# One more drain instruction on GpSimd, ahead of the last indirect scatter of an attention and mixture-of-experts kernel

## The chip, the cores and the metric

The kernel runs on one core of one Trainium2 chip. The metric is the device time of the program in microseconds; lower is better. A change is compared with the kernel before on the same chip.

## What is computed

Attention for 8 batches of 8 heads, 1152 keys of width 64 and 576 queries (each the mean of two neighbouring query rows), followed by a mixture of 8 experts on the 4608 tokens of width 512 that come out. Each token goes to one expert, the one with the largest gate.

```python
q_pool = q.reshape(B, H, S // 2, 2, D).mean(axis=3)
attn = softmax(scale * q_pool @ k.T)          # per batch and head
x = (attn @ v)                                # as 4608 rows of 512
logits = x @ w_gate + modality_bias[modality_id]
e_idx = argmax(logits);  gate_w = softmax(logits)[e_idx]
for e in range(8):
    rows = e_idx == e
    out[rows] = gate_w[rows] * (relu(x[rows] @ w1[e]) @ w2[e])
```

## The kernel before

**Two phases.** `attention` goes through 32 pairs of heads and writes the 4608 rows of x to a DRAM tensor `xs`, together with the gate and a scale of each row. `Router` works out for each row its expert and makes two lists of row numbers for blocks of 256 rows that belong to one expert: `giA`, `siA` for the first six blocks and `giB`, `siB` for the others. `experts` then works block by block.

**A block.** `load_x` gathers its rows from `xs` with two indirect DMAs of 128 rows each (`gather_x`, line 1173). These are issued by GpSimd (POOL), as are all indirect DMAs of the kernel. `load_w` fetches the expert's weights through SyncE's queue, `split_w` splits each weight piece into a high and a low half (ScalarE and VectorE, lines 1268 and 1269), `gemm1` and `gemm2` are the two matrix products on TensorE, `scaled` multiplies the result by the gate on ScalarE (`o`, line 1339), and `scatter` writes 128 rows of `o` to the rows of the output that `siA` or `siB` names, with an indirect DMA on GpSimd (line 1342).

**The order.** `run_blocks` writes out 18 full blocks by hand, all engines of the phase in the order of the code (`manual_schedule`). The first half of a block is scattered at its end (`scatter(j, 0)`), the second half five steps into the next block. After the loop stand the second half's scatter of the last full block (`scatter(order[-2], 1)`) and the split of the last weight piece. Then comes `block(NBF)`, a half block of 128 rows: `half_gemm1` makes the first product with rows and columns exchanged and turns it back with transposes (lines 1304 to 1316), `gemm2` makes the second (lines 1331 to 1333), `scaled` and `scatter` follow. That scatter is the last indirect DMA of the program.

**What is queued on GpSimd at the end.** In order: the two scatters of the last full block, the scatter of the half block, a load of a count from SBUF and a branch on it (lines 1426 and 1427; the count is 0 here, so the blocks of the conditional part are passed over), waits until every software-issued DMA has landed, one INC_SWDGE_SEM, which sets the semaphores of the software DMAs to what the passed-over branch would have left, and the program's end (line 1541): a drain on every engine, a barrier of all engines, a clearing of semaphores and a second barrier. Apart from this end, the only drain on GpSimd stands in the program's first microsecond (line 1533).

Of the kernel before, what the change touches and what calls it, by code (L numbers as in the profile page):

```python
# [156 lines left out]
def drain(g):  # L157
    for _ in g:
        pass
# [998 lines left out]
def index(rt, j, h):  # L1158
    (gi, si), k = (rt.idxA, 2 * j) if j < NA else (rt.idxB, 2 * (j - NA) if j < NBF else 2 * (NBF - NA) + j - NBF)
    return gi[:, k + h:k + h + 1], si[:, k + h:k + h + 1]  # L1160
# [38 lines left out]
def experts(tc, ctx, rt, ident, pre, w1, w2, out, side, first):  # L1199


    nc = tc.nc
# [20 lines left out]
    def load_x(j):  # L1223
        B.setdefault(j, {})["xg"] = gather_x(nc, rt, j, lambda h: xq.tile([P, XW], F32, name=f"xg{h}", bufs=1))

    def turn_x(j):

        b = B[j]
        b["gate"] = xp.tile([P, 2], F32, name="gate", bufs=3)
        b["xh"], b["xl"] = (xq.tile([P, 2, 4, P], F16, name="xpart", bufs=6) for _ in range(2))  # L1230
        for h in parts(j):
            x, sc = b["xg"][h][:, 0:DM], b["xg"][h][:, DM + 1:XW]
            nc.vector.tensor_copy(b["gate"][:, h:h + 1], b["xg"][h][:, DM:DM + 1])
            xh, xl = (xq.tile([P, DM], F16, name="xs", bufs=4) for _ in range(2))
            nc.scalar.activation(xh, x, AF.Copy, scale=sc)
            nc.vector.scalar_tensor_tensor(xl, x, sc, xh, op0=ALU.mult, op1=ALU.subtract)
            b["xs", h] = xh, xl
        yield
        for h in parts(j):
            for o, x in zip((b["xh"], b["xl"]), b["xs", h]):  # L1240
                nc.sync.dma_start_transpose(out=o[:, h], in_=x)
        yield

    def load_w(j, q):

        b = B.setdefault(j, {})
        e = b.get("e")
        if e is None:
            own, k = (rt.ownA, j) if j < NA else (rt.ownB, j - NA) if j < NBF else (rt.ownH, j - NBF)
            e = b["e"] = nc.sync.value_load(own[0:1, k:k + 1], min_val=0, max_val=E - 1)  # L1250
        if q < 4:
            t = wr.tile([P, 4, TB], F32, name="w1r", tag="w")
            nc.sync.dma_start(out=t.rearrange("p c f -> p (c f)"), in_=w1[bass.ds(e, 1), q].rearrange("a p n -> p (a n)"))
        else:
            t = wr.tile([P, 2, DM], F32, name="w2r", tag="w")
            nc.sync.dma_start(out=t.rearrange("p c f -> p (c f)"), in_=w2[bass.ds(e, 1), q - 4].rearrange("a p n -> p (a n)"))
        b["r", q] = t

    def split_w(j, q):
        b = B[j]  # L1260
        t = b["r", q]
        shape, nm = ([P, 4, TB], "w1") if q < 4 else ([P, 2, DM], "w2")
        if q < 4:
            i = next(slot) % W1B
            hi, lo = (pre.tile(shape, F16, name=f"{nm}{x}{i}") if i < NF else wp1.tile(shape, F16, name=nm + x) for x in "hl")
        else:
            hi, lo = (wp2.tile(shape, F16, name=nm + x) for x in "hl")
        nc.scalar.activation(hi, t, AF.Copy, scale=WSC)
        nc.vector.scalar_tensor_tensor(lo, t, WSC, hi, op0=ALU.mult, op1=ALU.subtract)
        b["w", q] = (hi, lo)  # L1270
# [65 lines left out]
    def scaled(j, h):  # L1336
        b = B[j]
        o = b["o", h] = xp.tile([P, DM], F32, name=f"o{h}")
        nc.scalar.activation(o, b["po"][h], AF.Copy, scale=b["gate"][:, h:h + 1])

    def scatter(j, h):
        nc.gpsimd.indirect_dma_start(out=out[:, :], out_offset=bass.IndirectOffsetOnAxis(ap=index(rt, j, h)[1], axis=0),  # L1342
                                     in_=B[j]["o", h][:, :], in_offset=None, bounds_check=T - 1, oob_is_err=False)
# [16 lines left out]
    def run_blocks():  # L1360

        todo = iter(pieces[NF:])

        def fetch(n=1):
            for _ in range(n):
                p = next(todo, None)
                if p:
                    load_w(*p)

        fetch(WR)  # L1370
        load_x(1)
        for q in range(NF, 4):
            split_w(0, q)
        turn = {1: turn_x(1)}
        fetch(4)
        late = order.index(NA)
        ahead, own = {}, {}
        for m in range(1, len(order)):
            own[m] = T_OWN[m == late] if m in (1, late) else ()
            ahead[m] = () if m in (1, late) else T_AHEAD  # L1380
        for i, j in enumerate(order[:-1]):
            for s in range(8):
                k = 8 * i + 7 + s
                if i == 0 and s < 4:
                    split_w(0, 4 + s)
                    fetch()
                (gemm1 if s < 4 else gemm2)(j, s % 4)
                for _ in range(own[i + 1].count(s)):
                    next(turn[i + 1], None)
                if k > 7:  # L1390
                    split_w(*pieces[k])
                    fetch()
                if i and s == T_ST:
                    scatter(order[i - 1], 1)
                if i + 2 < len(order) and i + 2 != late:
                    if s == GX:
                        load_x(order[i + 2])
                        turn[i + 2] = turn_x(order[i + 2])
                    for _ in range(ahead[i + 2].count(s)):
                        next(turn[i + 2])  # L1400
            drain(turn[i + 1])
            scaled(j, 0)
            scaled(j, 1)
            scatter(j, 0)
            if i + 2 == late:
                drain(side)
                load_x(order[i + 2])
                turn[i + 2] = turn_x(order[i + 2])
        scatter(order[-2], 1)
        split_w(*pieces[-1])  # L1410

    def block(j):
# [10 lines left out]
    with tc.manual_schedule(engines=MAN0):  # L1423
        run_blocks()
        block(NBF)
# [120 lines left out]
```

## Time and profile before

| | us |
|---|---|
| median of three runs | 1149.84 |
| lowest, highest | 1148.15, 1151.22 |
| the profiled execution, its own time | 1147.58 |
| its span, from the first to the last instruction | 1145.8 |
| outside the span in that execution | 1.78 |

The profile names an engine's sequencer with a q (POOLq): its instructions (waits, branches, drains) occupy the engine's queue but not the engine. A row of a view by source line gives an operation, how often it ran, the shortest, median and longest duration in ns, and the start of the first and of the last one in us from the span's start.

### The profile page before, as it was taken

The page shows a single profiled execution, that of the slowest core. Times are in us where ns is not written, and L with a number is a line of the kernel's source. Part 1 is how long each engine was busy: PE and PEld are TensorE (multiplying, and loading weights), DVE is VectorE, ACT ScalarE, POOL GpSimd, SP SyncE. Part 2 cuts the span into 40 slices and gives each one's busy share as a digit, 9 for nine tenths or more (in the row PEclk, how much of TensorE's full clock was granted, in tenths as well). Part 3 has the DMA queues.
Part 4 walks back from the last instruction along what each step waited for, and adds up shares of the span by engine and source line. Part 5 has one row for each costly group of instructions (what it writes and reads, how often), then busy time and mean ns, then how long its engine had stood idle before and what let it go on. Part 6 is the DMA issues. An engine that isn't in the chain of part 4 may idle for free. (4 is left out here: it accounts for less than half of the span.)

```text
span 1145.8 us, 36648 instructions
## 1 busy us (share of the span) xinstructions
PE 1109.3 (97%) x15001; PEld 816.3 (71%) x15001; DVE 978.9 (85%) x1962; ACT 915.3 (80%) x1463; POOL 419.5 (37%) x408
## 2 busy tenths in 40 slices
PE   7999999999999999999999989999999999999995
PEld 3777777777777777777777767866676666766763
DVE  7999999999999999999999999888977667576661
ACT  5999999999999999999999989765656565565561
POOL 7753534444343454434445331232213221211201
PEclk9999999999999999999999999999999999999998
DMA  7776867857858759669668453699989999989970
GB/s 230 204 178 166 190 178 166 196 158 165 194 148 201 190 149 206 152 164 207 165 167 186 129 129 85 226 269 273 287 259 294 291 289 275 280 267 289 263 233 22
DMA packets 175568, 232.65 MB, mean 203 GB/s; under 512 B 92351, under 2 KB 126799, under 8 KB 175392
## 3 DMA queue, kind: packets, MB, share of 16 engines
q1 hardware_dynamic: 169254, 210.45, 70.3%
q0 software_dynamic: 6128, 19.78, 6.4%
q8 instruction: 119, 1.95, 0.7%
q14 instruction: 57, 0.47, 0.2%
q10 hardware_dynamic: 10, 0.00, 0.0%
HBM read 146.11 MB, written 19.18 MB: 144 GB/s over the span
## 5 line engine op out<-in xcount | busy, mean ns | idle before, releaser
L881 ACT ACTIVATE Pe<-psc 128x432 int32<-128x432 f32 x768 | 377.9, 526 | 43.1 <-PE psc L880 34.2
L813 DVE TENSOR_REDUCE mp<-pm 128x1 f32<-128x512 f32 x566 | 372.6, 684 | 14.4 <-PE pm L812 7.2
L938 PE MATMUL xp<-VH,Pe 128*128 128x65 f16 x2880 | 372.6, 193 | 0.0
L940 PE MATMUL xp<-VS,Pl 128*128 128x65 f16 x2880 | 371.9, 193 | 0.4 <-DVE Pl L864 0.4
L939 PE MATMUL xp<-vl,Pe 128*128 128x64 f16 x2880 | 370.7, 192 | 0.0
L939 PEld LDWEIGHTS <-Pe 128*128 128x128 f16 x2880 | 267.6, 98 | 87.6
L879 PE MATMUL psc<-B 128*128 128x432 f16 (+2 forms) x1152 | 304.0, 286 | 1.7 <-ACT Pe L881 1.5
L880 PE MATMUL psc<-B 65*128 65x432 f16 (+2 forms) x1152 | 304.7, 287 | 0.5 <-DMA B<-mr 0.5
L938 PEld LDWEIGHTS <-Pe 128*128 128x128 f16 x2880 | 271.9, 98 | 45.2 <-issue 7.0
L940 PEld LDWEIGHTS <-Pl 128*128 128x128 f16 x2880 | 266.5, 97 | 0.6 <-DVE Pl L864 0.5
L862 ACT ACTIVATE Pl<-Pe 128x1152 f16<-128x1152 uint16 (+1 forms) x190 | 219.3, 1154 | 6.0
L812 PE MATMUL pm<-hi,QB 128*128 128x512 f16 x566 | 213.7, 379 | 8.4 <-DVE mp L813 8.1
L674 POOL TENSOR_TENSOR lo<-rawk,hi 128x576 f16<-128x576 f32 (+1 forms) x68 | 88.0, 1298 | 196.0 <-ACT hi L658 185.6
L761 POOL TENSOR_SCALAR VH<-rawv,sc 128x512 f16<-128x512 f32 (+1 forms) x60 | 103.5, 1735 | 153.0 <-PE xp L940 73.7
L1287 PE MATMUL ph<-xpart,w1l 128*128 128x256 f16 x544 | 148.3, 273 | 0.0
L1285 PE MATMUL ph<-xpart,w1h 128*128 128x256 f16 x544 | 148.3, 273 | 0.0
L1286 PE MATMUL ph<-xpart,w1h 128*128 128x256 f16 x544 | 148.3, 273 | 0.0
L880 PEld LDWEIGHTS <-B 65*128 65x128 f16 x1152 | 112.9, 98 | 25.2 <-issue 2.5
L879 PEld LDWEIGHTS <-B 128*128 128x128 f16 x1152 | 112.5, 98 | 9.2 <-issue 3.8
L1291 DVE SCALAR_TENSOR_TENSOR hl<-ph,hh 128x512 f16<-128x512 f32 x72 | 49.7, 690 | 77.0 <-ACT hh L1290 76.3
L1290 ACT ACTIVATE hh<-ph 128x512 f16<-128x512 f32 x72 | 43.0, 598 | 87.2 <-PE ph L1287 87.2
L1333 PE MATMUL po<-w2h,hl 128*128 128x512 f16 x296 | 112.2, 379 | 0.0
(263 smaller groups left out, 1921.2 us busy)
## 6 DMA issues: line engine op xcount, KB each, us to landing
w2r<-in_w_dram SPq DMA_DIRECT2D x76, 512.0 KB
w1r<-in_w_dram SPq DMA_DIRECT2D x72, 512.0 KB
rawv<-in_att_dram SPq DMA_DIRECT2D x32, 576.0 KB
B<-hi SPq DMA_DIRECT2D x128, 144.0 KB
rawq<-in_att_dram SPq DMA_DIRECT2D x31, 576.0 KB
rawk<-in_att_dram SPq DMA_DIRECT2D x31, 576.0 KB
B<-qh SPq DMA_DIRECT2D x128, 72.0 KB
B<-lo SPq DMA_DIRECT2D x64, 144.0 KB
```

The lines of the kernel that those rows point to most:

```text
L812: nc.tensor.matmul(pm, QB[p % 2][:, u], s["hi"][:, t * 512:(t + 1) * 512], start=True, stop=True)
L813: nc.vector.tensor_reduce(mp[:, u, t:t + 1], pm, op=ALU.max, axis=AX.X)
L862: nc.scalar.activation(low, rest, AF.Copy, scale=LOW)
L879: nc.tensor.matmul(o, b1[:, ks], b1[:, qs], start=True, stop=False, skip_group_check=True)
L880: nc.tensor.matmul(o, b2[:, ks], b2[:, qs], start=False, stop=True, skip_group_check=True)
L881: nc.scalar.activation(Pe[:, D + x0:D + x1], pt, AF.Exp, scale=1.0 / 16)
L938: nc.tensor.matmul(out, Ph[:, qs], vh[:, c, j, 0:D + 1], start=c == 0 and g == 0, stop=False, skip_group_check=True)
L939: nc.tensor.matmul(out[:, 0:D], Ph[:, qs], vl[:, c, j], start=False, stop=False, skip_group_check=True)
L940: nc.tensor.matmul(out, Pl[:, qs], vs[:, c, j, 0:D + 1], start=False, stop=c == NKC - 1, skip_group_check=True)
L1285: nc.tensor.matmul(o, hi[:, c, fs], xh[:, :, c], start=c == 0, stop=False)
L1286: nc.tensor.matmul(o, hi[:, c, fs], xl[:, :, c], start=False, stop=False)
L1287: nc.tensor.matmul(o, lo[:, c, fs], xh[:, :, c], start=False, stop=c == 3)
```

## The change

After the second half's scatter of the last full block, GpSimd gets one drain. It is written between two statements that stand there already:

```diff
         scatter(order[-2], 1)
+        nc.gpsimd.drain(fusable=False)
         split_w(*pieces[-1])
```

`split_w` issues nothing on GpSimd, so in GpSimd's queue the drain stands directly behind that scatter and directly in front of what belongs to the half block's scatter (a register move, a wait for the landing of the scatter in front, and the transfer itself). The drain waits for no semaphore and updates none. No other instruction of GpSimd or of another engine is added, removed or moved, and no wait changes its semaphore or its value. Line numbers behind the place rise by one: the program's end is line 1542 there, and the count and its branch are lines 1427 and 1428.

## Prediction

> **What bounds the kernel now.** I read the busy times by stage first, with the borders put where the half block begins and where its last work ends.
>
> ```profile
> core 0: us, PE busy (x) PEld busy (x) DVE busy (x) ACT busy (x) POOL busy (x), PEclk, DMA share, GB/s
> 0.00:700.00 700.00, 681.72 (x11499) 520.73 (x11500) 667.19 (x1487) 647.12 (x1098) 325.96 (x321) 1.00 0.71 173
> 700.00:1120.00 420.00, 415.97 (x3425) 287.88 (x3424) 308.76 (x471) 263.13 (x355) 90.64 (x85) 1.00 0.94 263
> 1120.00:1134.00 14.00, 11.59 (x81) 7.72 (x79) 2.92 (x5) 5.02 (x12) 2.34 (x3) 1.00 0.11 41
> 1134.00:1145.80 11.80, 0.00 (x0) 0.00 (x0) 0.00 (x0) 0.00 (x0) 0.59 (x1) 0.65 0.01 3
> ```
>
> TensorE is busy for 682 of the first 700 us and for 416 of the next 420. So the bulk is bound by TensorE, and a GpSimd instruction can do nothing for it. The last row is different: for 11.8 us no engine computes, apart from 0.59 us on POOL, and almost nothing moves (3 GB/s). Here the end of the program is set by queues alone, and that stretch is the one to take apart.
>
> The instructions of POOL and ACT around it, in order of time (start, duration):
>
> ```profile
> 1123.92 0.97 POOL L1342 DMA_INDIRECT out_dram<-o,siB  x1 [2.52 <-ACT hh L1306]
> 1133.61 0.97 POOL L1342 DMA_INDIRECT out_dram<-o,siB  x1 [8.72 <-ACT o L1339]
> ...
> 1132.65 0.69 ACT L1339 ACTIVATE o<-po,gate 128x512 f32<-128x512 f32 x1 [4.86 <-PE po L1333]
> ```
>
> The last scatter is issued at 1133.61, after `o` is ready at 1132.65 + 0.69 = 1133.34. Between the end of the scatter in front (1123.92 + 0.97 = 1124.89) and 1133.34 POOL has nothing to do: 8.45 us. What follows the last scatter on the sequencers stands in the views of two lines, the branch (L1427) and the program's end (L1541):
>
> ```profile
> L1427 POOLq EVENT_SEMAPHORE  x5: 17/43/1421, 1134.9 to 1136.6; - x5
> ...
> L1427 POOLq INC_SWDGE_SEM  x1: 1720/1720/1720, 1136.7 to 1136.7; - x1
> ...
> L1541 SPq EVENT_SEMAPHORE  x14: 17/28/28, 1138.4 to 1145.7; - x14
> L1541 POOLq EVENT_SEMAPHORE  x4: 17/17/17, 1144.8 to 1145.7; - x4
> L1541 POOLq DRAIN  x3: 40/107/6286, 1138.5 to 1145.3; - x3
> L1541 SPq DRAIN  x3: 7/7/13, 1139.1 to 1145.0; - x3
> L1541 DVEq DRAIN  x2: 17/72/128, 1132.1 to 1145.4; - x2
> L1541 PEldq DRAIN  x2: 8/8/8, 1133.7 to 1145.1; - x2
> L1541 ACTq DRAIN  x2: 8/8/8, 1136.5 to 1145.0; - x2
> ...
> L1541 POOLq EVENT_SEMAPHORE_RANGE_CLEAR  x1: 177/177/177, 1145.1 to 1145.1; - x1
> ```
>
> In order of time: POOL's waits for the landings, the longest 1.421 us, end at 1136.6; INC_SWDGE_SEM takes 1.720 us from 1136.7 and ends at 1138.4; then comes the first of POOL's three drains, from 1138.5. It must be the one of 6.286 us: POOL's first semaphore instruction of the end starts at 1144.8 = 1138.5 + 6.3, and the two later drains lie in the 1.0 us behind it. All other engines had come to their first drain long before: DVE at 1132.1, PE at 1133.7, ACT at 1136.5, SP at 1139.1. The barrier waits for POOL's drain alone. It is 6.286 us on the path that ends the program, 0.55% of the span, with no engine at work.
>
> **What the drain does in that time.** It doesn't wait for a transfer: all landings were waited for by 1136.6, in front of it. It doesn't wait for an instruction of the engine either, since POOL's last one ended at 1133.61 + 0.97 = 1134.6. And it isn't the price of a drain as such, since the next two take 0.107 and 0.040 us. The fourth drain of POOL in the program stands at its beginning, before any DMA:
>
> ```profile
> L1533 POOLq INC_SWDGE_SEM  x1: 31/31/31, 0.2 to 0.2; - x1
> ...
> L1533 POOLq DRAIN  x1: 169/169/169, 0.4 to 0.4; - x1
> ```
>
> 0.169 us. So the long one is the only drain that has software DMAs behind it which no drain has yet followed. These are the transfers issued by POOL:
>
> ```profile
> xs<-x POOLq DMA_DIRECT2D x1, 576.0 KB, 7.5
> ...
> xg<-xs,giB POOLq DMA_INDIRECT x25, 5.8
> out_dram<-o,siB POOLq DMA_INDIRECT x25, 5.3
> out_dram<-o,siA POOLq DMA_INDIRECT x12, 6.0
> xg<-xs,giA POOLq DMA_INDIRECT x10, 5.8
> ...
> rawq<-xs,giA POOLq DMA_INDIRECT x2, 6.8
> ...
> xs<-gt POOLq DMA_DIRECT2D x1, 9.0 KB, 6.8
> ```
>
> 1 + 25 + 25 + 12 + 10 + 2 + 1 = 76. My theory: a drain on POOL goes through a record of each software DMA that it hasn't closed before, and the end pays for what has gathered: 6.286 / 76 = 0.083 us each, if all 76 are still there (more each, if some were closed on the way).
>
> **The change, part by part.** It adds one instruction on POOL; nothing else is issued, removed or moved. Two costs and two gains come from it.
>
> *The new drain itself.* It stands behind the scatter that ends at 1124.89. Bounds for its length are the shortest drain, 0.040 us, and the long one, 6.286 us. I take 6.286, because 75 of the 76 transfers lie in front of it, as in the row of the long one. Queued behind it on POOL is only the last scatter with its register move and wait; who waits for that is the end of the program. If the drain starts at 1124.9, it ends at 1131.2, and `o` is ready at 1133.34: hidden, with 2.1 us left. It may first have to see the scatter in front landed, and the chain that ended last shows when POOL's queue saw that:
>
> ```profile
> 1123.92 2.73 DMA out_dram<-o,siB
> 1126.65 0.02 issue
> 1126.67 0.02 POOLq L1342
> 1126.69 6.69 issue
> 1133.38 0.02 POOLq L1426
> ```
>
> The wait for that landing passed at 1126.67. A drain that starts there ends at 1126.7 + 6.3 = 1133.0, still 0.3 us before 1133.34. So it costs nothing on the path: the cover is TensorE's second product of the half block and `o`, and each microsecond beyond the cover would come back in full.
>
> *The long drain at the end.* By the theory it has one record left, so it becomes as short as a drain with little to do: 0.107 us, the median of the three. Then it is not the last any more: SP is next. SP's drains of the first barrier begin at 1139.1 and it has three of 7 to 13 ns, the second of them about 0.1 us behind the first. POOL would be through at 1138.5 + 0.1 = 1138.6, the barrier waits for SP until about 1139.3 and not for POOL until 1144.8. The gain is 1144.8 - 1139.3 = 5.5 us, which is less than the 6.2 us taken from the drain, because SP's chain behind the last semaphores (12 waits at some 60 ns, from 1138.4 to 1139.1) now ends last.
>
> *INC_SWDGE_SEM.* SP's first wait of the end is over at 1138.4, just when INC_SWDGE_SEM ends, so both POOL and SP hang on that one. It took 1.720 us here and 0.031 at the program's beginning, where no software DMA had been issued. If it too works through what has gathered, the new drain shortens it, and all of what it saves is on the path. Bounds: saving nothing, and saving 1.720 - 0.031 = 1.7 us. The row at the beginning has no semaphores to raise, so it is a far bound, and the row at the end has all the records, which is as far; I take the middle, 0.8 us.
>
> *The instructions behind.* They stand one place later in POOL's queue; I cost that at nothing, because the branch, the waits and the end are reached after a wait for `o` of several us, which hides the fetch of one instruction.
>
> *The sum.* 5.5 + 0.8 = 6.3 us off. Against the profiled execution: 1147.58 - 6.3 = 1141.3 (span 1139.5, with the same 1.78 outside). That execution lies 2.26 us under the median of the three runs, 1149.84, and 0.57 under the lowest of them. Measured times are compared with such medians, so the forecast stands on that one: 1149.84 - 6.3 = 1143.5.
>
> Here a page speaks against the change. The rows of the end show drains of 7 to 128 ns on SP, ACT, PE and DVE, and one of 6,286 ns on POOL. The Trainium skill (VectorE: DVE Perf Modes, section "The DRAIN you can't avoid") says that the drains which frame a program are a constant of about 12 ns on all five engines. By that the sum would be zero, there being nothing to shorten; POOL's row of 6,286 ns contradicts it for this engine, and the measurement decides.
>
> **The rivals.**
>
> *The long drain isn't about what gathered (no change).* Its 6.286 us could be a fixed price of the first drain behind any software DMA, or belong to the last scatter or to INC_SWDGE_SEM, the instruction directly in front of it. All of these are still there after the change, and the new drain's own price is hidden: 1149.8. For it: the trace has a single long drain, so whether the cost is fixed or gathers can't be read from it, and a drain might clear nothing at all while the scatter in front is under way. Against it: the last scatter had landed 2 us before the drain, and INC_SWDGE_SEM has a row of its own, of 1.720 us, which was over. Nor does POOL need 6 us after a DMA before it can go on, as two gathers in a row show:
>
> ```profile
> 1059.21 0.99 POOL L1173 DMA_INDIRECT xg<-xs,giB  x1 [0.30 <-issue]
> 1060.50 0.97 POOL L1173 DMA_INDIRECT xg<-xs,giB  x1 [0.30 <-issue]
> ```
>
> They start 1.3 us apart. The Trainium skill (PSUM — Partial Sum Buffer, section "Engine vs sequencer instructions") says that a drain waits until its engine is fully idle. By that alone each drain waits for its own predecessors, and this rival holds; the trace, with POOL's last instruction over at 1134.6, shows no work of the engine to wait for. Chance 0.18.
>
> *Half of it gathers (a small gain).* If some of the 6.286 us is fixed, say half, 3.1 us stay at the end and POOL stays last in the barrier: 1149.84 - 3.1 = 1146.7. That is 0.27%, under what a measurement here can tell from no change, about 0.3% or 3.4 us. Chance 0.06.
>
> *The new drain is late (slower).* Its place is POOL's queue between 1124.9 and 1133.34. If it begins only at the landing (1126.67), takes the price of the end in full, with INC_SWDGE_SEM's share 1.72 + 6.29 = 8.0 us, and leaves the end as it was, the last scatter goes out at 1134.7 at the earliest and not at 1133.4: 1.3 us later, 1151.1. It decides from a length of 6.7 us behind the landing on; slower by over 0.3% needs 6.7 + 3.4 = 10.1 us, 1.6 times the longest drain of the trace. Against it: two things have to come together, a drain that costs more than it does at the end, where more transfers lie behind it, and an end that is no shorter. Chance 0.04, three quarters of it beyond 0.3%, since once such a drain costs more than the one at the end, no row bounds it from above.
>
> **How the numbers follow.** The forecast has what is left, 0.72. Its own range: gains from 5.5 us (INC_SWDGE_SEM as before) to 5.5 + 1.7 = 7.2 us, and the spread of the three runs about their median, from 1148.15 to 1151.22, that is 1.7 down and 1.4 up: 1149.84 - 7.2 - 1.7 = 1140.9 to 1149.84 - 5.5 + 1.4 = 1145.7. To hold 8 in 10 the range goes up over the half case at 1146.7 (0.72 + 0.06 = 0.78) to the lowest run of the no-change case, 1148.2. Faster by over 0.3% is the forecast alone, 0.72; within 0.3% are no change, the half case and a quarter of the late one, 0.18 + 0.06 + 0.01 = 0.25; slower is 0.03.
>
> **What would show it.** Right: in the views of the new drain's line and of the end, a drain of some 6 us from about 1125 on, the last scatter still issued at 1133.6, POOL's first drain of the end at about 0.1 us, and SP's first drain as the last before the barrier. INC_SWDGE_SEM under 1.7 us would confirm that term; at 1.72 the gain is 5.5. Wrong: a long drain at the end still (then the cost is fixed or belongs to what stands behind the new drain), or a last scatter issued after 1133.7 (then the cover was too short). If the new drain is short and the end's long, it cleared nothing.

## The result, and the profile after

| | before | with the drain |
|---|---|---|
| median of six runs, us | 1149.16 | 1141.18 |
| lowest, highest | 1148.15, 1151.22 | 1139.51, 1142.49 |
| profiled execution, its own time | 1147.58 | 1140.92 |
| its span | 1145.8 | 1139.2 |

The ratio is 0.9931, with a 95% interval from 0.992 to 0.9942: 8.0 us less.

The busy times by stage, with the same borders (the span ends earlier):

```profile
0.00:700.00 700.00, 682.48 (x11492) 520.88 (x11493) 666.51 (x1487) 646.62 (x1097) 325.08 (x321) 1.00 0.71 173
700.00:1120.00 420.00, 415.75 (x3428) 287.97 (x3427) 309.49 (x471) 263.65 (x356) 91.37 (x85) 1.00 0.94 263
1120.00:1134.00 14.00, 12.40 (x85) 8.11 (x82) 2.92 (x5) 5.40 (x12) 1.94 (x2) 1.00 0.11 40
1134.00:1139.20 5.20, 0.00 (x0) 0.00 (x0) 0.00 (x0) 0.15 (x1) 0.97 (x1) 0.69 0.04 10
```

The first two stages are what they were (TensorE 682.5 and 415.8 us), and in the third TensorE has 0.8 us more only because everything lies 0.8 us later here against the same borders. The stretch in which almost nothing computes has shrunk, from 11.8 to 5.2 us. Now the chain that ended last, the issues of POOL and the last `o`:

```profile
1124.50 1.19 POOLq L1410
1125.70 6.24 issue
1131.94 0.03 POOLq L1342
1131.97 0.05 issue
1132.02 0.02 POOLq L1342
1132.03 2.16 issue
1134.20 0.02 POOLq L1427
```

```profile
1124.73 0.97 POOL L1342 DMA_INDIRECT out_dram<-o,siB  x1 [2.51 <-ACT hh L1306]
1134.43 0.97 POOL L1342 DMA_INDIRECT out_dram<-o,siB  x1 [8.73 <-ACT o L1339]
```

```profile
1133.47 0.69 ACT L1339 ACTIVATE o<-po,gate 128x512 f32<-128x512 f32 x1 [4.86 <-PE po L1333]
```

L1410 is the new drain. POOL's queue comes to it at 1124.50 and goes on at 1131.94. The last scatter is issued at 1134.43, that is 0.27 us after `o` is ready (1133.47 + 0.69 = 1134.16), and before the change it was also 0.27 us (1133.61 - 1133.34). So the drain is hidden whole, with 2.2 us to spare. That all times here lie 0.8 us later than before isn't the drain's doing: the scatter at 1120.43 before, well ahead of it, starts at 1121.24 here. The sequencers' rows of the three lines (the new drain, the branch, the end):

```profile
L1410 POOLq DRAIN  x1: 7403/7403/7403, 1124.5 to 1124.5; - x1
...
L1428 POOLq INC_SWDGE_SEM  x1: 203/203/203, 1137.2 to 1137.2; - x1
...
L1542 SPq EVENT_SEMAPHORE  x14: 17/28/28, 1137.4 to 1139.1; - x14
L1542 POOLq EVENT_SEMAPHORE  x4: 17/17/17, 1138.2 to 1139.1; - x4
L1542 POOLq DRAIN  x3: 46/107/153, 1137.5 to 1138.7; - x3
L1542 SPq DRAIN  x3: 7/7/13, 1138.1 to 1138.4; - x3
```

The end's long drain is gone: 6.286 us before, 0.153 now. INC_SWDGE_SEM went from 1.720 to 0.203 us. POOL is through with its first drain at 1137.5 + 0.153, and its barrier starts at 1138.2, just behind SP's first drains at 1138.1. SP is the last now.

The account from the last scatter's issue on, as far as the rows go: issue to the start of INC_SWDGE_SEM, 3.1 us before (1133.61 to 1136.7) and 2.8 now; INC_SWDGE_SEM, 1.7 and 0.2; from its end to the barrier, 6.4 (1138.4 to 1144.8) and 0.8 (1137.4 to 1138.2); the barriers, 1.0 and 1.0. That is 12.2 against 4.8 us, 7.4 less. The span became only 6.6 shorter, as the 0.8 us in the bulk went the other way.

### The profile page after: what moved, and what is told of

Its sections match the earlier page's. It is cut to its first block, busy times and chain, and to the rows that moved or that the text cites. A ratio compares the mean times of both kernels' runs of the same rounds, so it can differ in the third digit from the quotient of the medians.

```text
span 1139.2 us, 36649 instructions
## 1 busy us (share of the span) xinstructions
PE 1110.6 (97%) x15001; PEld 817.0 (72%) x15001; DVE 978.9 (86%) x1962; ACT 915.8 (80%) x1463; POOL 419.4 (37%) x408
```

## The experiments

Two questions: does the cost gather with every software DMA, or is it a fixed price of a drain; and does it matter that the drain stands where other work covers it? The theory is the prediction's: a drain closes a record of each software DMA that no drain has closed before. The rivals: a fixed price paid once, a price of the last few transfers, or one more instruction at this place.

### Eight runs

**The changed kernel once more**, unchanged:

> The changed kernel once more, as the measure for the others: 8 us under before if the first comparison holds, 6.3 us if the forecast's sum is the truth and the rest was scatter between runs.

Measured: 1140.73 us against 1148.01, ratio 0.9937 (0.9924 to 0.995), 7.2 us by the ratio. The end is the same to the nanosecond:

```profile
L1410 POOLq DRAIN  x1: 7403/7403/7403, 1124.1 to 1124.1; - x1
L1428 POOLq INC_SWDGE_SEM  x1: 203/203/203, 1136.9 to 1136.9; - x1
L1542 POOLq DRAIN  x3: 46/107/153, 1137.1 to 1138.4; - x3
```

The forecast's 6.3 us (0.9945) lies within this interval, and 8 us within it too; these runs don't tell the two apart. The interval of the first comparison (6.7 to 9.2 us) leaves 6.3 us just outside. The trace's account, below, says which terms differ.

**One drain in the middle**, in block 9, instead of the one at the end:

```diff
                 if i and s == T_ST:
                     scatter(order[i - 1], 1)
+                    if i == 9:
+                        nc.gpsimd.drain(fusable=False)
...
         scatter(order[-2], 1)
-        nc.gpsimd.drain(fusable=False)
```

> One drain on POOL in block 9, none ahead of the last scatter: 44 software DMAs lie in front of it, 32 behind it. If records gather (0.083 us each, from 6.286 us for 76): this drain works 44 x 0.083 = 3.6 us, the end's drain 32 x 0.083 = 2.6 us, INC_SWDGE_SEM falls in proportion, 0.2 + 31 x 0.020 = 0.8 us; the time is 3.6 + 0.9 = 4.5 us under before. If a drain has a fixed price paid once: some 6 us here and 0.15 at the end, 7 to 8 us under before. If only the last few transfers count (a store that holds fewer than 32): 6.3 at the end and no gain.

Measured: 1143.36 us, ratio 0.9956 (0.9943 to 0.9969), so 5.1 us under before by the ratio, with 4.5 expected.

```profile
L1396 POOLq DRAIN  x1: 7445/7445/7445, 939.8 to 939.8; - x1
L1429 POOLq INC_SWDGE_SEM  x1: 840/840/840, 1137.1 to 1137.1; - x1
L1543 POOLq DRAIN  x3: 46/107/2676, 1138.0 to 1141.2; - x3
```

The end pays for the 32 transfers behind the drain: 2.676 us, with 2.6 expected, and 0.840 for INC_SWDGE_SEM, with 0.8 expected. A fixed price would have left 0.15, a store of the last few 6.3. The drain in the middle took 7.4 us and not 3.6. It stands right behind a scatter, whose own rows are these:

```profile
L1342 POOL DMA_INDIRECT out_dram<-o,siB x1: 1537/1537/1537, 940.0 to 940.0; - x1
...
DMA to landing us min/median/max: 5.4/5.4/5.4
```

The scatter's issue ends at 941.5, it lands (its data have arrived) at 940.0 + 5.4 = 945.4 us, and the drain ends at 939.8 + 7.4 = 947.2, that is 1.8 us behind the landing. The next two experiments show what that means.

**A drain in every block**, and the one at the end:

```diff
                 if i and s == T_ST:
                     scatter(order[i - 1], 1)
+                    nc.gpsimd.drain(fusable=False)
```

> A drain behind the second half's scatter of every block, and the one of the changed kernel. If records gather: each closes 2 to 6 transfers, so 0.2 to 0.5 us of work behind the wait for the scatter in front (about 1.2 us); the end as in the changed kernel, and the time the same within 0.5 us, since POOL is idle for over 10 us a block. If a drain has a fixed price: some 6 us each, which delays the gathers behind it and could cost time. If spreading the work frees the scatters of their long issues (up to 3.6 us): the same time, but shorter scatters.

Measured: 1141.61 us, ratio 0.9943 (0.993 to 0.9956): as the changed kernel within the intervals (the medians are 0.9 us apart, at most 0.5 was expected, and these runs do not resolve that). The lengths of the drains were not as expected:

```profile
L1395 POOLq DRAIN  x17: 3732/5915/9117, 772.3 to 1104.1; - x17
...
L1411 POOLq DRAIN  x1: 3071/3071/3071, 1123.7 to 1123.7; - x1
```

With 2 to 12 transfers each, the work is 0.2 to 1.0 us, but a drain took 5.9 us in the median. The last of them shows why: it has 2 transfers, starts at 1123.7 and ends at 1126.8, just when the scatter in front of it had landed in the trace of before (1126.65, the same scatter, issued at 1123.92 in both traces). The view of the output's scatters in the same run has their times from issue to landing (the first and the second halves' together):

```profile
DMA to landing us min/median/max: 2.7/5.6/8.5
```

The drains, 3.1 to 9.1 with 5.9 in the median, follow them, a few tenths of a us more. Taken one by one, 17 of the 18 have the landing of the scatter in front in the trace, and each of these ends behind it: by 0.1 to 0.3 us with 2 to 6 transfers, by 0.5 with 12. So a drain on POOL waits for that landing (whether for this transfer alone isn't told apart, since it was the last to land wherever the trace has the landing of the one before). With few records this wait is nearly all of its time; with 75, in the changed kernel, the scatter landed at 1127.4 (1124.73 + 2.7), while the old records were worked through. Nor did it free the scatters: the longest issue of them still took 3.5 us here.

```profile
L1342 POOL DMA_INDIRECT out_dram<-o,siA x12: 971/1019/3467, 765.1 to 878.3; - x12
```

**The one drain a block earlier**, in block 17:

```diff
                 if i and s == T_ST:
                     scatter(order[i - 1], 1)
+                    if i == NBST - 1:
+                        nc.gpsimd.drain(fusable=False)
...
         scatter(order[-2], 1)
-        nc.gpsimd.drain(fusable=False)
```

> The one drain stands behind the second half's scatter of the last but one full block, 73 transfers in front and 3 behind. If records gather: 73 x 0.083 = 6.0 us of work there, 0.3 us at the end, INC_SWDGE_SEM 0.25 us: the same time as the changed kernel within 0.5 us. If the place directly ahead of the last scatter matters: slower than the changed kernel by up to the 8 us.

Measured: 1141.31 us, ratio 0.9938 (0.9925 to 0.995): the changed kernel's within the intervals. The place directly ahead of the last scatter isn't special.

```profile
L1396 POOLq DRAIN  x1: 8137/8137/8137, 1107.7 to 1107.7; - x1
L1429 POOLq INC_SWDGE_SEM  x1: 260/260/260, 1139.9 to 1139.9; - x1
L1543 POOLq DRAIN  x3: 46/107/316, 1140.2 to 1141.5; - x3
```

Three transfers are left: 0.316 us, with 0.3 expected. The drain itself took 8.1 us, where 1.2 us until the scatter's issue ended and 6.0 of work make 7.2. Its scatter was slow to land, as the one in the middle was:

```profile
L1342 POOL DMA_INDIRECT out_dram<-o,siB x1: 971/971/971, 1107.9 to 1107.9; - x1
...
DMA to landing us min/median/max: 4.9/4.9/4.9
```

It landed at 1112.8 and the drain ended at 1115.8, 3.0 us later. That is the work of 37 records out of 73, and in the middle 1.8 us was that of 22 out of 44; behind 12 transfers 0.5 us is that of 6. So about half of the record work comes behind the landing, however long that took. By this reading a drain ends half its work behind the later of two times, the landing and the middle of the work; in the changed kernel the landing came first and cost nothing. The reading was made from these traces afterwards, no run was made to test it, and why it is half stays open.

**The drain without cover**, behind the last scatter:

```diff
         run_blocks()
         block(NBF)
+        nc.gpsimd.drain(fusable=False)
...
         scatter(order[-2], 1)
-        nc.gpsimd.drain(fusable=False)
```

> The drain stands behind the last scatter, in front of the load of the count, with nothing to cover it. If what counts is that the work lies under other work: it takes 1.2 us of waiting for the scatter plus 6.3 us, the landing (3 us) passes meanwhile, the end's drain is 0.1 us, INC_SWDGE_SEM 0.2 us, and the end comes only 1 to 2 us earlier than before. If one more drain by itself makes the end cheap: 7 to 8 us under before, as in the changed kernel.

Measured: 1146.53 us, ratio 0.9989 (0.998 to 0.9998): 1.3 us under before, where 1 to 2 were expected.

```profile
L1426 POOLq DRAIN  x1: 7495/7495/7495, 1133.4 to 1133.4; - x1
L1428 POOLq INC_SWDGE_SEM  x1: 189/189/189, 1142.9 to 1142.9; - x1
L1542 POOLq DRAIN  x3: 34/50/107, 1143.1 to 1144.4; - x3
```

The end is as cheap as it gets (the first drain 0.050 us, with no transfer left), and still nearly all of the gain is lost, because the 7.5 us of the added drain now lie on the path. The added drain is as long as expected (1.2 + 6.3 us). What was gained by the change was its cover, not a cheaper total: work of some 6 us was moved under TensorE. From the last scatter's issue (1133.6 in both traces) to the start of INC_SWDGE_SEM it is 9.3 us here and was 3.1 before: the drain until 1140.9, which the landing passes beneath, and 2.0 us for the count, the branch and the waits. Behind that start 1.9 us are left (1142.9 to the span's end at 1144.8) and 9.1 were before.

**A memset in the drain's place:**

```diff
         scatter(order[-2], 1)
-        nc.gpsimd.drain(fusable=False)
+        nc.gpsimd.memset(xq.tile([P, 1], F32, name="none", bufs=1), 0.0)
```

> At the drain's place stands a memset of 128x1 on POOL. If the drain's own work matters: no change, 6.3 us at the end, INC_SWDGE_SEM 1.7 us. If one more instruction at this place (a shifted queue, an awake engine) does it: some of the 8 us gained.

Measured: 1147.61 us, ratio 0.9999 (0.999 to 1.0008): nothing.

```profile
L1428 POOLq INC_SWDGE_SEM  x1: 1720/1720/1720, 1135.9 to 1135.9; - x1
...
L1542 POOLq DRAIN  x3: 40/107/6286, 1137.6 to 1144.5; - x3
```

Same end, to the nanosecond. One more instruction in this place does nothing.

**Fewer and more transfers, with no drain added.** First without the second half's scatter of 17 blocks:

```diff
                 if i and s == T_ST:
-                    scatter(order[i - 1], 1)
```

> No drain added; the second half's scatter of the first 17 blocks is left out, so these rows of the output are not written: 59 software DMAs instead of 76. If records gather: the end's drain 59 x 0.083 = 4.9 us, INC_SWDGE_SEM 1.4 us. If the price is fixed or goes by the last transfers alone: 6.3 and 1.7 us.

Then with each scatter of the full blocks issued twice:

```diff
                 if i and s == T_ST:
                     scatter(order[i - 1], 1)
+                    scatter(order[i - 1], 1)
...
             scatter(j, 0)
+            scatter(j, 0)
```

> No drain added; each scatter of the full blocks is issued twice (the same rows with the same values), 111 software DMAs instead of 76. If records gather without limit: the end's drain 111 x 0.083 = 9.2 us, INC_SWDGE_SEM 2.4 us. If the store is limited or the price fixed: 6.3 and 1.7 us.

```profile
L1425 POOLq INC_SWDGE_SEM  x1: 1380/1380/1380, 1137.3 to 1137.3; - x1
L1539 POOLq DRAIN  x3: 40/107/4897, 1138.7 to 1144.2; - x3
```

```profile
L1429 POOLq INC_SWDGE_SEM  x1: 580/580/580, 1177.2 to 1177.2; - x1
L1543 POOLq DRAIN  x3: 40/107/1631, 1177.8 to 1180.0; - x3
```

59 transfers: 4.897 us, with 4.9 expected. The second was a miss for every theory: 111 transfers, 1.631 us where 9.2 or 6.3 were expected. (Its time, 1182.21 us, tells nothing on this: each doubled scatter waits for its twin to land.) On the line that the other runs make, 1.631 us is 19 records, so something had closed 92 of the 111 on the way, without a drain. INC_SWDGE_SEM gives the same count: 0.580 = 0.260 + 16 x 0.020, 16 more than the three of the run a block earlier. (The kernel with 59 ran once, in 1146.65 us; nothing is read from that time.)

### Two runs on the miss

Is there a store of about 92 that empties itself, or does something else close them, in time or in the waits? The first half's scatter was doubled in 11 blocks, and in all 18:

```diff
             scatter(j, 0)
+            if i < 11:
+                scatter(j, 0)
```

```diff
             scatter(j, 0)
+            scatter(j, 0)
```

> No drain added; the first half's scatter of the first 11 blocks is issued twice: 87 software DMAs. The earlier run with 111 of them ended with 1.631 us, which is (1.631 - 0.071) / 0.0818 = 19 records, so something closed 92 on the way. If that happens when a store of about 92 is full: nothing has been closed here, the end's drain is 0.071 + 87 x 0.0818 = 7.19 us and INC_SWDGE_SEM 0.183 + 87 x 0.0202 = 1.94 us. If it happens by time or by waits instead (the doubled scatters wait for each other): less than that, 1 to 3 us.

> No drain added; the first half's scatter of all 18 full blocks is issued twice: 94 software DMAs. If a store of 92 is emptied at once when it is full: 2 records at the end, 0.23 us of drain and 0.22 us of INC_SWDGE_SEM. If a full store only closes as many as it needs: about 92 at the end, 7.6 and 2.0 us. If it goes by time or waits: a figure between.

```profile
L1429 POOLq INC_SWDGE_SEM  x1: 1940/1940/1940, 1139.1 to 1139.1; - x1
L1543 POOLq DRAIN  x3: 40/107/7184, 1141.1 to 1148.9; - x3
```

```profile
L1428 POOLq INC_SWDGE_SEM  x1: 2080/2080/2080, 1142.3 to 1142.3; - x1
L1542 POOLq DRAIN  x3: 40/107/7756, 1144.4 to 1152.7; - x3
```

With 87 transfers the drain took 7.184 us (7.19 expected). With 94 it took 7.756: 0.071 + 94 x 0.0818 = 7.76, so all 94 were still there, and a store of 92 that empties itself at once is refuted. Eighteen doubled scatters and their waits don't close records. In the kernel with 111 transfers, 35 of them doubled, something does; what it is, and whether it goes by the number, the time or the waits, stays open. (Each of the two ran once, in 1151.02 and 1154.88 us against 1148.26 before; only the lengths at the end are read from them.)

### The line

| transfers not yet closed | drain, us | INC_SWDGE_SEM, us | kernel |
|---|---|---|---|
| 0 | 0.050 | 0.189 | without cover |
| 1 | 0.153 | 0.203 | changed |
| 3 | 0.316 | 0.260 | a block earlier |
| 32 | 2.676 | 0.840 | in the middle |
| 59 | 4.897 | 1.380 | fewer scatters |
| 76 | 6.286 | 1.720 | before |
| 87 | 7.184 | 1.940 | 11 doubled |
| 94 | 7.756 | 2.080 | 18 doubled |

From 3 to 76 the drain grows by (6.286 - 0.316) / 73 = 0.0818 us each and INC_SWDGE_SEM by (1.720 - 0.260) / 73 = 0.020. From 76 to 94 it is 1.470 / 18 = 0.0817 and 0.020. Both are straight lines in the number of software DMAs since the last drain, in eight kernels. With few transfers the drain is off its line by some 0.02 us: 0.050 with none, where the line gives 0.071, and 0.134 with one in the run with a drain in every block, against 0.153.

What the line doesn't show is whether the cost goes by the transfer or by what is in it. All but two of the 76 transfers are indirect ones of 128 rows, and no run changed their size.

## Why the prediction was right

The mechanism is the one put down, and its steps are found in the trace. One term was too small.

- **What bounds the end.** POOL's drain, which waits for no transfer there. Shown: a change of nothing but POOL's drains moves the time, a memset doesn't.
- **The records.** 6.286 / 76 = 0.083 us each was the estimate; the line gives 0.0818 and about 0.07 us for a drain by itself. That nothing had been closed on the way, which the prediction left open, holds here, and up to 94.
- **The new drain, 6.286 us, hidden.** It took 7.403: 1.2 us until the scatter in front had been issued (1124.50 to 1125.70), then 6.21 for 75 records, 0.083 each. Counted from the scatter's end that is the 6.3 us forecast, and of the cover 2.2 us were left, with 2.1 forecast.
- **The end's drain.** 5.5 us by SP taking over as the last. Measured from INC_SWDGE_SEM's end to the barrier: 6.4 - 0.8 = 5.6.
- **INC_SWDGE_SEM.** This is the mis-sized term. Between its two bounds, 0 and 1.7 us, the middle was taken, 0.8; it saved 1.720 - 0.203 = 1.5, almost the whole. The same count rules it, so the row at the program's beginning was the near bound. What it does to semaphores no run shows, only how long it takes.
- **The sum.** 5.6 + 1.5 = 7.1 us in place of 6.3; with 0.3 us by which the stretch up to INC_SWDGE_SEM was shorter (the last scatter took 2.6 us to land instead of 2.9), which no term foresaw, the tail makes 7.4. The two comparisons gave 8.0 and 7.2. Of the distance from the 1143.5 us forecast to the 1141.18 measured, 0.7 us is the median of before, which fell from 1149.84 with three runs to 1149.16 with six.
- **No change (0.18)** fell with the drain in the middle, which left 32 records' worth at the end, and with 59 transfers. The Trainium skill's rule that stood behind it (PSUM — Partial Sum Buffer, section "Engine vs sequencer instructions"), that a drain waits for its engine to be idle, is borne out as far as it goes, by the 1.2 us behind the scatter, but says nothing of the 6.2 us that follow. The Trainium skill's constant of about 12 ns on all five engines (VectorE: DVE Perf Modes, section "The DRAIN you can't avoid") holds for none of POOL's drains here: 34 to 7,756 ns at the end.
- **Half of it (0.06)** fell too: what is fixed is 0.05 to 0.07 us.
- **Late (0.04).** Its condition, a drain that waits for the landing, is real: the drains in every block show it. But that wait runs beside the first half of the record work, so with the 2.7 us landing here it added nothing. Where the landing took 4.9 and 5.4 us it added 0.9 and 2.0 us (8.1 instead of 7.2, 7.4 instead of 5.4), so by the same reading a landing of 5.4 us at this place would have taken 1.3 of the 2.2 us of cover, an estimate (1124.73 + 5.4 = 1130.1, where the middle of the work was at 1128.8). The end that stays as long, the rival's other condition, was seen with no drain of this kind: a drain put on the path, in the experiment without cover, lost most of the gain and was still no slower than before.

## What to carry to other kernels

Where a program issues many DMAs from GpSimd, look at the length of GpSimd's drain at the end, in the sequencer's rows, not in the busy times: it grows with the number of such DMAs since the last drain, and at the end nothing covers it. One drain in an idle stretch of GpSimd, near the end but with as much cover ahead of the next needed transfer as the records take (0.08 us each in this kernel's variants, and 1 to 2 us more where the transfer in front is slow to land), moves that cost under other work. The same drain without cover gives almost nothing, and drains in between give no more than the last one does.

## What was not expected of the hardware

A drain on POOL that stands behind an indirect scatter waits for its landing: 3.1 to 9.1 us with 2 to 12 transfers to close. About half of its record work comes behind that landing: 1.8 us of it with 44 transfers and 3.0 with 73. INC_SWDGE_SEM takes 0.020 us for each software DMA that no drain has closed, besides 0.19 for itself. And in one kernel records were closed without a drain: 111 transfers left 19, where 94 had left all 94.
